# One expert block's gathers placed later in the GpSimd order, and a narrower rule for which PSUM accesses need no order

## The chip, the cores and the metric

The kernel runs on one core of one Trainium2 chip. The metric is the device time of one execution in microseconds (us). Three runs of the kernel before gave 913.91, 916.37 and 916.81 us, the median being 916.37 us.

## The reference

Attention comes first: 8 batches, 8 heads, 576 tokens of 64 dimensions, with rotary embedding on q and k. Its output, laid out as 4608 tokens of 512 values, goes through a mixture of 8 experts that picks one expert a token:

```python
scores = scale * np.matmul(q_rot, k_rot.transpose(0, 1, 3, 2))
attn = np.exp(scores - max); attn = attn / (sum + 1e-09)
x = (attn @ v).transpose(0, 2, 1, 3).reshape(4608, 512)
logits = x @ w_gate + modality_bias[modality_id]
e_idx = np.argmax(logits, axis=1); gate_w = softmax(logits)[e_idx]
for e in range(8):
    h = np.maximum(x[e_idx == e] @ w1[e], 0.0)        # 512 -> 1024
    out[e_idx == e] = gate_w * (h @ w2[e])            # 1024 -> 512
```

## The kernel before, in words

**Attention.** The 64 heads are worked as 32 pairs of heads, numbered 0 to 31, four pairs to a batch (so batch 5, the sixth in time, is pairs 20 to 23). A pair has nine score units S0 to S8. Each is a set of fp32r matmuls on TensorE into one PSUM slot (`scores`, matmul at L472), a pass of VectorE that copies the scores and takes the row minimum (`rowmin`, L481), and an exponential on ScalarE (`expo`, L490). The exponentials are then transposed on TensorE into PSUM by six fills: F0, F1, F2, F3, FA, FB (`fill`, `tpose`, L495). `evac` copies every fill out: the half g = 0, which is the first PSUM bank of the slot, on ScalarE (`acopy`, L432), the half g = 1, the second bank, on VectorE (`tensor_copy` at L528). F0 and F1 go to PH[0], F2 and F3 to PH[1], FA to PD[0]; FB is three copies an engine, into PH[1] and PD[1]. `AV` (L553) multiplies by V, half 0 (AVA) from PH[0], half 1 (AVB) from PH[1]. `avout` copies the result, `outp` (OUT, L590) turns it and computes the routing logits, `ev` (L603 to L607) scales it on VectorE.

**PSUM.** Attention has four slots, SL[0] to SL[3], each one tile of two banks. The table SLOTS says which unit takes which: F1 and F3 slot 3, F2 and S5 slot 0, F0, S8, S0 and OUT slot 1, FA, FB and S1 slot 2. `take` takes both banks of a slot (or one, for AV) and `give` hands a bank back.

**Which instructions wait for which.** The scheduler looks at the tiles that an instruction reads and writes and makes it wait for earlier instructions on other engines with which it shares a tile. `alone(own, b, inst)` is called by `evac`, `AV`, `avout` and `ev` for each access to bank b of slot `own`. It goes through the accesses recorded since the slot was taken, and for each of the other bank and of another engine it calls `declare_no_dep` with the reason "two banks": these two need no order.

**Order.** Every piece of work is a job with a key. The tables KEYS, EDGE (pairs with an order of their own: 0 to 4 and 26 to 31, and parts of 5 and 25) and MOE give the keys, and 14.438 times the pair is added. Jobs are sorted by key, and TensorE, ScalarE, VectorE, GpSimd and the DMA queue of SyncE each execute their instructions in that order. MOE's keys count from pair 31.

**Routing.** For each batch `route` picks the expert of each token; its last step casts the table rows `oi` on GpSimd (L697). `scatter` (L708) then writes a batch's token numbers and gates into TAB in DRAM, in five indirect DMAs of GpSimd, SC0 to SC4. Batches 0 to 4 make a first plan (`plan0`), in PLA: 8 expert blocks of 256 tokens that can begin before attention ends. `m_plan` loads a block's expert, row and flag from the plan into registers of SyncE (L932 to L934). `m_ix` issues two loads of the block's rows of TAB (ix at L944, xi at L946). `m_gather` computes addresses once a block (iy, L962) and issues eight indirect DMAs of GpSimd (L970) that fetch the tokens from X in DRAM into XG[s % 2]. A block's XG is transposed on VectorE (`m_tr`, L1015), split in high and low parts (`m_tre`), multiplied by w1 (`m_l1`, L1034), and by w2 (`m_l2`, L1053), and stored by an indirect DMA (L1057).

**Around the change.** Block 0's gathers run among pair 31's attention. Before the change block 1's plan values, index loads and gathers come next. On GpSimd its eight gathers stand directly behind block 0's last one, with the multiplication of `route` (L689) between them, and ahead of the cast `oi` of batch 5 and its five scatters, in the order SC3, SC4, SC2, SC1, SC0.

Of the kernel before, what the change touches and what calls it, by code (L numbers as in the profile page):

```python
# [194 lines left out]
MOE = dict(  # L195
    setdma=(-353.070, -199.654, -64.082, -129.156),
    consts=(28.166, 28.282),
    plan=(-34.727, 11.672, -5.857, -25.884),
    ix=(-13.525, 11.677, 11.679, 11.775),
    w1=(-33.501, -27.735, 15.231, -22.655),  # L200
    w2=(-4.011, 1.762, 12.647, -8.483),
    hi=(-22.046, 1.027, 19.870, 16.903),
# [6 lines left out]
    l1e=(22.809, 22.869, 24.662, 24.647),  # L209
    w1n=(20.502, 24.643, 23.254, 22.825),  # L210
    place=(10.490, 11.490),
    rows=(5.189, -7.595, 2.778, 1.170, -0.984, 8.071, 5.429, 11.766, 11.780, 11.790, 14.020, 14.030, 14.040, 14.050, 14.060, 14.070,
        25.150, 25.160, 25.170, 25.180, 25.190, 25.200, 25.210, 25.220),
    pl=(-114.356, -102.856, -99.906, -88.406, -85.506, -73.956, -51.417, -48.907, -45.303),
    end=25.0,
# [6 lines left out]
def tile_attention_moe(ctx: ExitStack, tc: tile.TileContext, qk, v, mod, wg, mb, w1, w2, rope, cf, ci, out):  # L222
    nc = tc.nc
# [75 lines left out]
    def take(nm, bks):  # L299

        own = SLOTS[nm]
        if nm == "RK8":
            own, bks = own & 3, (own >> 2,)
        if not all((own, b) in idle for b in bks):
            if nm == "RK8":
                own, b = min(idle, key=idle.get)
                bks = (b,)
            else:
                own = min((i for i in range(4) if all((i, b) in idle for b in bks)), key=lambda i: max(idle[i, b] for b in bks))
        for b in bks:  # L310
            del idle[own, b]
        if len(bks) == 2:
            use[own] = []
        return (own, *bks) if nm == "RK8" else own

    use = {}

    def alone(own, b, inst):

        for x, i in use[own]:  # L320
            if x != b and i.engine != inst.engine:
                tc.declare_no_dep(inst, i, reason="two banks")
        use[own].append((b, inst))

    def give(own, *bks):
        for b in bks:
            idle[own, b] = clock[0]
            clock[0] += 1
# [192 lines left out]
    def evac(n, f, g):  # L521
        d = st[n]
        ps = d[f][:, g]
        give(d["at", f], g)


        def cp(o, i):
            alone(d["at", f], g, (nc.vector.tensor_copy if g else acopy)(o, i).ins)  # L528

        if f[1] in "0123":  # L530
            h, o = divmod(int(f[1]), 2)
            o = o * P + g * 64
            cp(PH[h][:, :, o:o + 64], ps.rearrange("p (a b) -> p a b", b=64))
            return
        tails = PD[f == "FB"][:, 0:256].rearrange("p (j s c) -> p j s c", s=2, c=64)[:, :, g, :]
        if f == "FA":
            cp(tails, ps[:, 0:128].rearrange("p (j c) -> p j c", c=64))
        else:
            cp(PH[1][:, 4 * g:4 * g + 4, 256:320], ps[:, 0:256].rearrange("p (k c) -> p k c", c=64))
            cp(PD[1][g * 64:g * 64 + 64, 256:320], ps[g * 64:g * 64 + 64, 256:320])  # L540
            cp(tails, ps[:, 320:448].rearrange("p (j c) -> p j c", c=64))


    def AV(n, half):
        d = st[n]
        c0, c1 = (0, 256) if half == 0 else (256, 576)
        own = take("AV" + "AB"[half], (half,))
        pa = d["pa", half] = SL[own][:, half, :]
        d["at", "av", half] = own
        for kt in range(5):  # L550
            for hh in range(2):
                r = PH[half][:, 4 * hh + kt, :] if kt < 4 else PD[half]
                i = nc.tensor.matmul(pa[hh * 64:hh * 64 + 64, 0:c1 - c0], d["V"][:, hh, kt, :], r, start=(kt == 0), stop=(kt == 4))  # L553
                alone(own, half, i.ins)
                d.setdefault(("av", half), i.ins)

    def avout(n, half):
        d = st[n]
        c0, c1 = (0, 256) if half == 0 else (256, 576)
        own = d.pop(("at", "av", half))  # L560
        alone(own, half, acopy(OT[n % 2][:, c0:c1], d.pop(("pa", half))[:, 0:c1 - c0]).ins)
        give(own, half)
# [603 lines left out]
    for n in range(NPAIR):  # L1166
# [11 lines left out]
        for w in range(2):  # L1178
            c = "AB"[w]
            K_(f"AV{c}", AV, n, w)  # L1180
            K_(f"OT{c}", avout, n, w)
            K_(f"EV{c}", ev, n, 1 - w)
# [12 lines left out]
        if n % 4 == 3:  # L1195
            K_("BIAS", bias, n // 4)
            K_("XO", xout, n // 4)
            g = route(n // 4)
            steps = [(next, g, None)] * (NRK - (n == z))
            scats = [(scatter, n // 4, j) for j in range(5)]  # L1200
            if n == z:

                g = plan()
# [22 lines left out]
    g = plan0()  # L1226
# [201 lines left out]
```

## Time and profile before

| | us |
|---|---|
| median of three runs | 916.37 |
| the profiled execution's own time | 911.67 |
| its span, first to last instruction | 909.9 |
| TensorE busy | 863.7 |
| TensorE weight loads busy | 715.4 |
| VectorE busy | 685.8 |
| GpSimd busy | 641.1 |
| ScalarE busy | 632.3 |

The profile is one execution. PE is TensorE's matmuls, PEld its weight loads, DVE VectorE, ACT ScalarE, POOL GpSimd, SP SyncE with its DMA queue SPq. A row of the timeline gives start and length in us, the engine, the line of the kernel, the operation, the tiles as out<-in without their numbers, and the count of merged instructions; in brackets stands the idle time ahead of it with what ended that. "issue" there means that the engine waited for nothing that the profile shows. Attention lasts from the start to about 476 us, and the expert blocks from then to the end.

### The profile page before, as it was taken

What the parts mean: (1) busy time and instruction counts of PE and PEld (TensorE: products, weight loads), DVE (VectorE), ACT (ScalarE), POOL (GpSimd) and SP (SyncE); (2) the same over time, 40 slices, a digit from 0 to 9 for tenths busy, and PEclk for the clock granted to TensorE, in tenths of its full rate; (3) what the DMA queues carried; (4) which work ended last, traced back from release to release, by engine and by line L of the source; (5) the groups of instructions that cost most, each with busy time, mean ns of one, the idle gap of its engine ahead of it and who ended that gap; (6) DMA issues with size and microseconds to landing.
All of it is one profiled execution on the core that took longest, in us unless ns stands there. A gap on an engine that the chain in (4) does not pass through costs nothing. (4 is left out here: it accounts for less than half of the span.)

```text
span 909.9 us, 25743 instructions
## 1 busy us (share of the span) xinstructions
PE 863.7 (95%) x9696; PEld 715.4 (79%) x9696; DVE 685.8 (75%) x1515; ACT 632.3 (69%) x1291; POOL 641.1 (70%) x494
## 2 busy tenths in 40 slices
PE   2899999999999999999869989999999999999996
PEld 2677777777777777777648978889999999999995
DVE  7788889888888889888739767857676666666672
ACT  2888988888988988989734545556556555555563
POOL 3999988998889999995551776765666666666401
PEclk9999999999999999999969999999999999999999
DMA  8675778788797787867601611116717112511250
GB/s 263 200 225 156 247 180 219 182 207 204 151 246 181 190 207 182 230 166 215 171 21 67 222 49 46 54 59 228 237 55 229 47 47 88 192 46 38 81 171 20
DMA packets 82465, 136.90 MB, mean 150 GB/s; under 512 B 28795, under 2 KB 53517, under 8 KB 81308
## 3 DMA queue, kind: packets, MB, share of 16 engines
q1 hardware_dynamic: 71740, 114.08, 46.5%
q0 software_dynamic: 9248, 19.46, 6.6%
q8 instruction: 78, 1.28, 0.6%
q10 hardware_dynamic: 1344, 1.62, 0.6%
q14 instruction: 55, 0.45, 0.2%
HBM read 138.16 MB, written 19.51 MB: 173 GB/s over the span
## 5 line engine op out<-in xcount | busy, mean ns | idle before, releaser
L481 DVE CUSTOM_DVE_ANT_1 sc<-ps,ZERO 128x576 f32<-128x576 f32 x288 | 206.8, 749 | 23.3 <-PE ps L472 13.0
L490 ACT ACTIVATE P<-sc,mn 128x576 f32<-128x576 f32 x288 | 219.7, 767 | 5.8 <-DVE mn L481 5.2
L970 POOL DMA_INDIRECT XG<-X,iy x148 | 174.6, 1180 | 48.5 <-issue 37.6
L1034 PE MATMUL psH<-HL,W1H 128*128 128x256 f32 x1088 | 194.6, 281 | 3.2 <-issue 2.9
L472 PE MATMUL ps<-SW 64*128 64x288 f32 x960 | 170.3, 312 | 15.8 <-DMA SW<-HL 14.9
L472 PE MATMUL ps<-HL 64*128 64x288 f32 x960 | 170.6, 311 | 3.2 <-DVE ri L573 1.1
L1034 PEld LDWEIGHTS psH<-HL,W1H 128*128 128x128 f32 x1088 | 168.1, 189 | 4.0 <-issue 1.9
L1034 PE MATMUL psH<-HL,W1L 128*128 128x256 f32 x544 | 152.8, 281 | 0.9 <-issue 0.9
L472 PEld LDWEIGHTS ps<-SW 64*128 64x128 f32 x960 | 136.2, 190 | 20.6 <-DMA SW<-HL 15.9
L429 DVE TENSOR_TENSOR W1L<-ST,W1H 128x1024 fp32r<-128x1024 f32 x76 | 90.3, 1222 | 76.3 <-ACT W1H L432 65.5
L472 PEld LDWEIGHTS ps<-HL 64*128 64x128 f32 x960 | 136.2, 190 | 8.6 <-issue 5.5
L553 PE MATMUL ps<-PH,V 128*64 128x320 f32 (+1 forms) x1024 | 140.9, 416 | 2.2 <-issue 1.2
L1057 POOL DMA_INDIRECT out_dram<-sc,ix x36 | 47.0, 1305 | 115.3 <-ACT sc L1056 94.0
L495 PEld LDWEIGHTS ps<-idf,P 64*128 64x128 f32 x2624 | 96.8, 139 | 32.7 <-ACT P L490 12.1
L432 ACT ACTIVATE PH<-ps 128x512 f32<-128x512 f32 (+1 forms) x160 | 85.3, 551 | 48.5 <-PE ps L495 25.0
L528 DVE COPY PH<-ps 128x512 f32<-128x512 f32 (+1 forms) x160 | 98.4, 630 | 26.6 <-remote 12.8
L495 PE MATMUL ps<-idf,P 64*128 64x64 f32 x2624 | 109.1, 226 | 6.9 <-issue 3.5
L1053 PE MATMUL psY<-W2L,SW 128*128 128x512 f32 x288 | 113.7, 395 | 0.0
L1053 PE MATMUL psY<-W2H,SW 128*128 128x512 f32 x288 | 112.3, 390 | 0.0
L553 PEld LDWEIGHTS ps<-PH,V 128*64 128x64 f32 x1024 | 69.7, 137 | 51.3 <-issue 6.0
L449 POOL TENSOR_TENSOR HL<-ST,HL 128x1152 fp32r<-128x1152 f32 x31 | 82.4, 2657 | 36.6 <-ACT HL L432 36.5
L1034 PEld LDWEIGHTS psH<-HL,W1L 128*128 128x128 f32 x544 | 102.9, 189 | 3.8 <-issue 3.7
(216 smaller groups left out, 1596.7 us busy)
## 6 DMA issues: line engine op xcount, KB each, us to landing
ST<-in_moe_w_dram SPq DMA_DIRECT2D x152, 512.0 KB
ST<-in_qk_dram SPq DMA_DIRECT2D x62, 576.0 KB
SW<-HL SPq DMA_DIRECT2D x124, 216.0 KB
V<-in_v_dram SPq DMA_DIRECT2D x32, 256.0 KB
X<-X SPq DMA_DIRECT2D x8, 1024.0 KB
XG<-X,iy POOLq DMA_INDIRECT x148
V<-in_v_dram SPq DMA_DIRECT2D x64, 16.0 KB
X<-XT SPq DMA_DIRECT2D x16, 64.0 KB
```

What stands on the lines that cost most here:

```text
L429: nc.vector.tensor_tensor(o, a, b, op=ALU.subtract)
L432: return nc.scalar.activation(o, i, AF.Copy, scale=scale)
L449: e.tensor_tensor(d["HL"][:, 1, o], a, d["HL"][:, 0, o].bitcast(F32), op=ALU.subtract)
L472: nc.tensor.matmul(ps[:, g, 0:288], t[:, wq, q0:q0 + P], t[:, wk, k0:k0 + 288], start=(m == 0), stop=(m == len(L) - 1))
L481: nc.vector.tensor_tensor_reduce(sc, d.pop(("S", u))[:, :, 0:288], ZERO.unsqueeze(2).to_broadcast([P, 2, 288]), 1.0, FMAX, ALU.add, ALU.mi ...
L490: nc.scalar.activation(p, sc.rearrange("p a b -> p (a b)"), AF.Exp, bias=mn, scale=-1.0, accum_out=d["sum"][:, u:u + 1])
L495: nc.tensor.transpose(ps[:, g, c:c + 64], src[r, k0:k0 + P], idf[r, r])
L528: alone(d["at", f], g, (nc.vector.tensor_copy if g else acopy)(o, i).ins)
L553: i = nc.tensor.matmul(pa[hh * 64:hh * 64 + 64, 0:c1 - c0], d["V"][:, hh, kt, :], r, start=(kt == 0), stop=(kt == 4))
L970: inst = nc.gpsimd.indirect_dma_start(out=XG[s % 2][:, t, g, :], out_offset=None, in_=X.rearrange("n (i f) -> (n i) f", f=P)[0:rows], in_o ...
L1034: l1_[s] = nc.tensor.matmul(ps[:, i, :], w[:, c, f0:f0 + P], x[:, c, :], start=(m == 0), stop=(m == 11)).ins
L1053: nc.tensor.matmul(ps, hx[:, c, t * P:(t + 1) * P], x[:, c, :], start=(m == 0), stop=(m == 23))
```

## The change

Two things change. First, block 1's plan values move from key 11.672 to 16.183, its index loads from 11.677 to 17.300, and its eight gathers from 11.780 to 14.070 to 17.360 to 17.430. Batch 5's scatters stand at 15.355 (SC3), 16.855 (SC4), 17.438 (SC2), 21.457 and 22.004, counted in the same way. So on GpSimd the cast `oi` and two scatters come ahead of the eight gathers, and three scatters behind them; on SyncE's queue the plan values and the index loads come behind the index loads of blocks 2 and 3 and behind w1's third quarter of block 0 (15.231), and ahead of w1's first quarter for block 1 (20.502).

Second, `alone` takes a `part`, and no longer declares two accesses free of order when both have the same part. `evac` passes 0 for F0, F1 and FA, and 1 for F2, F3 and FB; `AV` passes its half; `avout` and `ev` pass none.

```diff
-    plan=(-34.727, 11.672, -5.857, -25.884),
-    ix=(-13.525, 11.677, 11.679, 11.775),
+    plan=(-34.727, 16.183, -5.857, -25.884),
+    ix=(-13.525, 17.300, 11.679, 11.775),
...
-    rows=(5.189, -7.595, 2.778, 1.170, -0.984, 8.071, 5.429, 11.766, 11.780, 11.790, 14.020, 14.030, 14.040, 14.050, 14.060, 14.070,
+    rows=(5.189, -7.595, 2.778, 1.170, -0.984, 8.071, 5.429, 11.766, 17.360, 17.370, 17.380, 17.390, 17.400, 17.410, 17.420, 17.430,
...
-    def alone(own, b, inst):
-
-        for x, i in use[own]:
-            if x != b and i.engine != inst.engine:
+    def alone(own, b, inst, part=None):
+
+        for x, p, i in use[own]:
+            if x != b and i.engine != inst.engine and (p is None or p != part):
                 tc.declare_no_dep(inst, i, reason="two banks")
-        use[own].append((b, inst))
+        use[own].append((b, part, inst))
...
-            alone(d["at", f], g, (nc.vector.tensor_copy if g else acopy)(o, i).ins)
+            alone(d["at", f], g, (nc.vector.tensor_copy if g else acopy)(o, i).ins, int(f[1] in "23B"))
...
-                alone(own, half, i.ins)
+                alone(own, half, i.ins, half)
```

## The prediction

> **What bounds the kernel now.** I read the page first (span, busy time, chain of waits), then the busy time of the attention stretch, then the timelines of the places that the diff touches.
>
> ```profile
> span 909.9 us, 25743 instructions
> ## 1 busy us (share of the span) xinstructions
> PE 863.7 (95%) x9696; PEld 715.4 (79%) x9696; DVE 685.8 (75%) x1515; ACT 632.3 (69%) x1291; POOL 641.1 (70%) x494
> ...
> q8 instruction: 78, 1.28, 0.6%
> ...
> PE 36%; issue 1%; POOL 1%; ACT 0%; DVE 0%; DMA 0%; POOLq 0%; ACTq 0%
> ```
> ```profile
> 97.00:355.00 258.00, 255.38 (x4172) 194.12 (x4171) 222.13 (x665) 227.23 (x585) 233.45 (x152) 1.00 0.81 196
> ```
>
> TensorE bounds it: 95% busy, and nearly all that the chain names. In the attention stretch from 97 to 355 us (pairs 5 to 23, 19 of them, so 13.6 us a pair) it is busy for 255.38 of 258.00 us, in full clock. The columns behind are weight loads, VectorE with 222.13 (86%) and ScalarE with 227.23 (88%). So there is no idle time on TensorE into which a new wait could sink: what delays its next matmul there is paid, unless it makes a later wait shorter.
>
> **The second edit: the two copies of a fill.** I take this one first because it acts in every pair. In `evac` both copies of a fill have the same slot, different banks, different engines, and now the same part, so the new test is false for every such pair and "two banks" is no longer declared. The declaration was there to take away an order: the two copies share the PSUM tile of the slot, though neither its banks nor the columns that they write. Without it I expect the later one in program order to wait for the earlier. It is the only thing that `declare_no_dep` can have removed between them. The keys say who is first: ScalarE in F0, F1, F2, FA and FB, VectorE in F3 (13.72 against 13.92).
>
> Here is one pair's crowded place, FB, F3 and F2, on ScalarE, then VectorE, then TensorE, each from its timeline:
>
> ```profile
> 306.39 0.26 ACT L432 ACTIVATE PD<-ps 128x128 f32<-128x128 f32 x1
> 306.56 0.60 ACT L432 ACTIVATE PH<-ps 128x512 f32<-128x512 f32 x1
> 306.56 1.09 ACT L432 ACTIVATE PH<-ps 128x512 f32<-128x512 f32 x2
> ```
> ```profile
> 306.00 0.42 DVE L528 COPY PH<-ps 128x256 f32<-128x256 f32 x1 [0.29 <-PE ps L495]
> 306.89 0.68 DVE L528 COPY PH<-ps 128x512 f32<-128x512 f32 x1
> 307.49 0.68 DVE L528 COPY PH<-ps 128x512 f32<-128x512 f32 x1
> 308.08 0.75 DVE L481 CUSTOM_DVE_ANT_1 sc<-ps,ZERO 128x576 f32<-128x576 f32 x1
> 308.76 0.08 DVE L481 DVE_READ_ACCUMULATOR2_ANT mn<- 128x1 f32 x1
> ```
> ```profile
> 307.72 0.71 PE L495 MATMUL ps<-idf,P 64*128 64x64 f32 x16
> 308.21 0.38 PE L472 MATMUL ps<-SW 64*128 64x288 f32 x1
> ...
> 309.12 0.29 PE L472 MATMUL ps<-SW 64*128 64x288 f32 x1
> ...
> 309.60 1.30 PE L553 MATMUL ps<-PH,V 128*64 128x320 f32 x8
> ```
>
> Now the copies run side by side. Walked again with the order put in, with 0.04 us for a release to arrive (VectorE's F2 copy ends at 307.49 + 0.68 = 308.17, and the next TensorE work starts at 308.21):
>
> - FB: ScalarE's third copy ends at 306.39 + 0.26 = 306.65, so VectorE's first starts at 306.69, not 306.00: 0.69 late.
> - F3: VectorE's copy moves from 306.89 to 307.58 and ends at 308.26. ScalarE's waits for it and starts at 308.30, not 306.56: 1.74 late. It ends at 308.90.
> - F2: ScalarE's copy follows in the old distance (1.09 for two, 0.60 for one, so 0.49 apart), at 308.79, to 309.39. VectorE's starts at 309.43, not 307.49: 1.94 late.
> - The minimum of S8 stands right behind it on VectorE: 308.08 becomes 310.02, and its result is out at 308.84 + 1.94 = 310.78.
> - TensorE: the next pair's F1 needs slot 3, which ScalarE's F3 copy leaves at 308.90, so 307.72 becomes 308.94 (1.22 late). The last scores of this group, S0, need slot 1, which the minimum of S8 frees: about 309.10 (one matmul ahead of the row at 309.12) becomes 310.82. That is 1.72 late, and AVB, at 309.60, is late with it.
>
> A second place is F0, whose slot OUT takes next:
>
> ```profile
> 300.72 0.58 ACT L432 ACTIVATE PH<-ps 128x512 f32<-128x512 f32 x1
> ```
> ```profile
> 300.78 0.69 DVE L528 COPY PH<-ps 128x512 f32<-128x512 f32 x1
> ```
> ```profile
> 301.62 0.60 PE L590 MATMUL ps<-RW,oT 64*64 64x72 f32 x23
> ```
>
> VectorE's copy would start at 301.34 and end at 302.03, and OUT at 302.07: 0.45 late at most. A TensorE that is late already gives ScalarE time to be there sooner, so I take 0.2. The copies of FA (0.26 us) and of F1 (VectorE comes there after the late minimum) I take at nothing: the work on VectorE ahead of them covers that; uncovered, F1's would cost one ScalarE copy, 0.6, and FA's 0.26, and they stay inside the upper bound of the other pairs below.
>
> Per pair 1.72 + 0.2 = 1.92 us. From below it is 1.22 (F1's fill alone, all else caught up), from above 1.72 + 0.45 = 2.17. Nineteen pairs have this order: 19 x 1.92 = 36.5 us (23 to 41). The other 13 have orders of their own (in pair 27 the keys set F0's copies 0.95 apart, for instance); there the bounds are 0 and 13 x 2.17 = 28, and I take a good quarter, 8, since their copies stand further apart. Sum of this edit: **+44.5 us**, bounds 23 and 69. The other new effect, AVB waiting for ScalarE's F3 copy, I cost at 0: AVB stands in the order behind F2's copies, which on ScalarE come after F3's in the usual order.
>
> By the Trainium skill, "PSUM — Partial Sum Buffer", section "Specifications (TRN2)", ScalarE and VectorE can read PSUM in parallel at full bandwidth as long as the bank differs. The rows at 300.72 and 300.78 agree. By that rule the chip needs no order here and the sum would be 0; but it is the program that waits.
>
> **The first edit: where the move lands.** Rows of TensorE around it, its usual pace for the same three pieces of work, then GpSimd, VectorE and SyncE's queue:
>
> ```profile
> 455.20 0.71 PE L590 MATMUL ps<-RW,oT 64*64 64x72 f32 x13
> ...
> 461.39 0.37 PE L590 MATMUL ps<-RW,oT 64*64 64x72 f32 x1 [1.05 <-issue]
> ...
> 473.09 0.76 PE L553 MATMUL ps<-PD,V 128*64 128x256 f32 x4
> ```
> ```profile
> 450.51 0.86 PE L590 MATMUL ps<-RW,oT 64*64 64x72 f32 x36
> 451.33 0.72 PE L495 MATMUL ps<-idf,P 64*128 64x64 f32 x16
> ```
> ```profile
> 303.00 1.95 PE L553 MATMUL ps<-PH,V 128*64 128x256 f32 x16
> 304.78 0.60 PE L553 MATMUL ps<-PD,V 128*64 128x256 f32 x4
> ```
> ```profile
> 451.13 0.99 POOL L970 DMA_INDIRECT XG<-X,iy  x1 [1.45 <-PE ps L590]
> 452.76 1.06 POOL L970 DMA_INDIRECT XG<-X,iy  x1 [0.27 <-POOL iy L962]
> ...
> 462.12 0.99 POOL L970 DMA_INDIRECT XG<-X,iy  x1 [0.30 <-issue]
> 463.12 0.20 POOL L697 CAST oi<-of 128x5 int32<-128x5 f32 x1
> 463.60 1.03 POOL L708 DMA_INDIRECT TAB<-VAL,oi  x1 [0.28 <-issue]
> ...
> 468.74 0.97 POOL L708 DMA_INDIRECT TAB<-VAL,oi  x1 [0.30 <-issue]
> 491.08 0.19 POOL L697 CAST oi<-of 128x5 int32<-128x5 f32 x1 [21.37 <-DVE of L694]
> ```
> ```profile
> 460.11 0.15 DVE L694 TENSOR_REDUCE of<-rk 128x5 f32<-128x40 f32 x1
> ...
> 492.74 1.28 DVE L1015 STREAM_TRANSPOSE XG<-XG 128x512 f32<-128x512 f32 x2
> ```
> ```profile
> 449.12 33.47 SPq L986 DMA_DIRECT2D ST<-in_moe_w_dram  x5
> ```
> ```profile
> L932 SPq TENSOR_LOAD <-PLA x4: 267/279/475, 404.5 to 442.0; - x4
> ```
>
> Moved past each other, the eight gathers and two scatters cost GpSimd the same 1.30 us each. The cast can start when `of` is there, at 460.26. Two scatters then end at about 463.2, the iy and eight gathers at 474, three scatters at 478, where they ended at 469.7. Block 1's tokens are first read at 492.74, 18 us later, and GpSimd's next work is at 491.08: both hide it, and without that cover each us late would be a us on the block 1 split. On SyncE three plan loads (0.28 each and registers) and two issues now stand behind the first w1 quarter of the row at 449.12 and ahead of one that waits until 477 anyway: nothing.
>
> What the move may change is the hole. OUT, a fill and AVA take 18.65 us from 455.20 to 473.85, where the usual pace is 0.86 + 0.72 + 2.38 = 3.96: **14.7 us are lost**, in "issue" time that names no releaser, while GpSimd issues one indirect DMA after another. After the move GpSimd has none between block 0's last gather at 451.13 + 0.99 and the cast. Whether the hole goes with the gathers the trace cannot say. Against it speaks a later stretch in which GpSimd (the fifth engine in the row, busy 15.95 of 20.00 us) gathers for another block:
>
> ```profile
> 500.00:520.00 20.00, 20.00 (x141) 18.29 (x140) 16.96 (x28) 12.95 (x17) 15.95 (x15) 1.00 0.73 238
> ```
>
> TensorE is busy in all of its 20.00 us. I take 0 and keep 0 to -14.7.
>
> By the Trainium skill, "Runtime: NRT & Kernel Launch", section "Instruction fetch mechanics", an engine refills its instructions in 16 KiB blocks by a DMA queue of its own; q8's 78 packets in 1.28 MB are such blocks. By that rule the hole would be TensorE's own and stay, and the sum would be +44.5; if it were the gathers', +29.8.
>
> **Sum.** 911.67 + 44.5 = 956.2 us for the profiled execution; the median of the runs stands 4.70 above that execution, so 960.9, said as 961.
>
> **The rivals.**
>
> - The hole closes as well: 961 - 14.7 = **946**. For it: the hole lies inside the run of gathers. Against: the stretch from 500 us, and that they only move some 8 us on, beside the first expert matmuls.
> - It ends on the other side if no wait comes with the copies, the scheduler telling the two banks apart by itself, and the hole closes: 916.4 - 14.7 = **902**. It decides from the point where the copies cost less than 14.7 / 32 = 0.46 us a pair. Against it: then the declaration in the kernel before would have had no use.
> - Neither happens, and the change does nothing: **916**.
> - The other 13 pairs pay in full and F0 too, 69 us: **986**.
>
> **How the numbers follow.** The forecast (copies wait, hole stays) 0.50, the hole closing as well 0.30, faster 0.07, no change 0.06, worse than 985 0.07. The forecast's own range is 940 to 985. The range of all that I hold to 8 in 10 takes in the second case, whose middle is 946 and which reaches down to some 936: 936 to 985. About 0.3% is what a measurement of this kernel can tell from no change. Faster by more than that: 0.08; within it: 0.05; slower: 0.87.
>
> **What would show it.** In the profile after, F3's copy on ScalarE starts after VectorE's has ended, F2's on VectorE after ScalarE's; the waits name DVE PH for ACT PH and the reverse; pairs 5 to 23 take about 15.5 us each and TensorE falls to some 87% in that stretch. The first edit is right if OUT and AVA of pair 31 take as long as now, wrong if they take 4 us. The whole is wrong if the two copies still start together.

## The result

The kernel after takes **961.74 us** in the median of four runs (952.75 to 964.91) beside 915.14 for the kernel before (908.49 to 916.81): a ratio of 1.0508, with a 95% interval of 1.0433 to 1.0583. It is slower. The profiled execution took 952.75 us, with a span of 951.0 where before had 909.9, so 41.1 us more.

From the page of the kernel after: the span, the busy time, the chain that ended last by engine, and two of the costliest groups, the copies of a fill on VectorE and on ScalarE (line, operation, count, then busy us and mean ns of one, then the idle time ahead of them and what ended most of it).

```profile
span 951.0 us, 25629 instructions
PE 878.1 (92%) x9696; PEld 714.9 (75%) x9696; DVE 687.5 (72%) x1515; ACT 639.2 (67%) x1291; POOL 654.4 (69%) x494
PE 74%; DVE 9%; ACT 8%; issue 5%; DMA 1%; POOL 1%; ACTq 0%; POOLq 0%; DVEq 0%
L528 DVE COPY PH<-ps 128x512 f32<-128x512 f32 (+1 forms) x160 | 100.7, 633 | 67.8 <-ACT PH L432 44.5
L432 ACT ACTIVATE PH<-ps 128x512 f32<-128x512 f32 (+1 forms) x160 | 85.1, 550 | 62.3 <-DVE PH L528 32.5
```

The same two groups in the kernel before:

```profile
L528 DVE COPY PH<-ps 128x512 f32<-128x512 f32 (+1 forms) x160 | 98.4, 630 | 26.6 <-remote 12.8
L432 ACT ACTIVATE PH<-ps 128x512 f32<-128x512 f32 (+1 forms) x160 | 85.3, 551 | 48.5 <-PE ps L495 25.0
```

The copies are as long as before (633 against 630 ns, 550 against 551). What is new is whom they wait for: VectorE's copies were held for 44.5 us by ScalarE's, ScalarE's for 32.5 us by VectorE's. And the chain goes 9% over VectorE and 8% over ScalarE. The chain of before that the prediction shows can't be laid beside it, since it reaches back only to 552.33 us, behind attention. In a second profile of before (below, on the first chip) the chain covers nearly the whole span, with 2% and 4% in the same two places:

```profile
PE 90%; ACT 4%; DVE 2%; DMA 1%; another core or an unknown queue 1%; issue 1%; ACTq 0%; POOLq 0%; POOL 0%; DVEq 0%
```

The same crowded place as in the prediction, FB, F3 and F2 of a pair, in the timelines of ScalarE, then VectorE, then TensorE of the kernel after:

```profile
344.45 0.38 ACT L432 ACTIVATE PH<-ps 128x256 f32<-128x256 f32 x1 [0.16 <-PE ps L495]
346.80 1.09 ACT L432 ACTIVATE PH<-ps 128x512 f32<-128x512 f32 x2 [1.69 <-DVE PH L528]
```
```profile
345.13 0.42 DVE L528 COPY PH<-ps 128x256 f32<-128x256 f32 x1 [0.87 <-ACT PD L432]
345.57 0.53 DVE L528 COPY PD<-ps 64x64 f32<-64x64 f32 x2
346.02 0.68 DVE L528 COPY PH<-ps 128x512 f32<-128x512 f32 x1
347.91 0.69 DVE L528 COPY PH<-ps 128x512 f32<-128x512 f32 x1 [1.21 <-ACT PH L432]
```
```profile
340.07 0.86 PE L590 MATMUL ps<-RW,oT 64*64 64x72 f32 x36 [0.37 <-DVE PH L528]
...
347.45 0.72 PE L495 MATMUL ps<-idf,P 64*128 64x64 f32 x16 [1.18 <-ACT PH L432]
...
349.94 2.37 PE L553 MATMUL ps<-PH,V 128*64 128x320 f32 x16
```

It reads as a staircase. ScalarE copies its part of FB, then VectorE its own (from 345.13), then VectorE F3 (346.02 to 346.70), then ScalarE F3 and F2 (346.80 to 347.89), then VectorE F2 (347.91). No two copies of one fill overlap any more. TensorE pays 1.18 us ahead of F1's fill and 0.37 ahead of OUT.

The second place is the stretch behind the last OUT but one, where before lost 14.7 us (TensorE of the kernel after):

```profile
512.85 1.48 PE L590 MATMUL ps<-RW,oT 64*64 64x72 f32 x36
514.26 0.80 PE L495 MATMUL ps<-idf,P 64*128 64x64 f32 x16
514.99 1.95 PE L553 MATMUL ps<-PH,V 128*64 128x256 f32 x16
516.76 0.60 PE L553 MATMUL ps<-PD,V 128*64 128x256 f32 x4
```

OUT, the fill and AVA take 4.5 us where they took 18.65. **The hole has closed.** (The prediction calls it pair 31's OUT; by the keys it is an earlier pair's, which changes nothing in the times.)

So the traces, laid against each other at the same pieces of TensorE's work, give in us:

| | before | after | difference |
|---|---|---|---|
| start to OUT of pair 4 | 97.7 | 100.7 | +3.0 |
| OUT of pair 4 to OUT of pair 23, 19 pairs | 258.2 | 302.3 | +44.1 |
| from there to the last OUT but one | 99.3 | 109.9 | +10.6 |
| from there to the first expert matmul | 21.3 | 7.1 | -14.2 |
| from there to the end | 433.4 | 431.0 | -2.4 |
| span | 909.9 | 951.0 | +41.1 |

The copies cost 57.7 us, 14.2 came back at the hole, and 2.4 behind it. The last figure hangs on this one trace of before: a second one took 426.3 us there in place of 433.4.

### The profile page after: what moved, and what is told of

Same layout as the page of the kernel before. It is cut to its first block, busy times and chain, and to the rows that moved or that the text cites. A ratio compares the mean times of both kernels' runs of the same rounds, so it can differ in the third digit from the quotient of the medians.

```text
span 951.0 us, 25629 instructions
## 1 busy us (share of the span) xinstructions
PE 878.1 (92%) x9696; PEld 714.9 (75%) x9696; DVE 687.5 (72%) x1515; ACT 639.2 (67%) x1291; POOL 654.4 (69%) x494
## 3 DMA queue, kind: packets, MB, share of 16 engines
q8 instruction: 78, 1.28, 0.6%
## 4 chain that ended last, share of the span: by engine, by line
PE 74%; DVE 9%; ACT 8%; issue 5%; DMA 1%; POOL 1%; ACTq 0%; POOLq 0%; DVEq 0%
PE psH L1034 20%; PE psY L1053 20%; PE ps L553 16%; PE ps L472 10%; DVE PH L528 6%; PE ps L495 5%; ACT PH L432 4%; PE ps L590 2%; ACT P L490 2%; DVE PD L528 1%; DVE sc L481 1%; POOL XG L970 1%; ACT PD L432 1%; PE psY L1094 1%; ACT HL L432 1%
## 5 line engine op out<-in xcount | busy, mean ns | idle before, releaser
L970 POOL DMA_INDIRECT XG<-X,iy x148 | 192.2, 1299 | 51.5 <-issue 36.9
L481 DVE CUSTOM_DVE_ANT_1 sc<-ps,ZERO 128x576 f32<-128x576 f32 x288 | 206.1, 748 | 15.5 <-PE ps L472 8.6
L472 PE MATMUL ps<-SW 64*128 64x288 f32 x960 | 184.3, 318 | 16.7 <-DMA SW<-HL 12.7
L472 PE MATMUL ps<-HL 64*128 64x288 f32 x960 | 185.0, 318 | 6.9 <-ACT PH L432 2.2
L528 DVE COPY PH<-ps 128x512 f32<-128x512 f32 (+1 forms) x160 | 100.7, 633 | 67.8 <-ACT PH L432 44.5
L429 DVE TENSOR_TENSOR W1L<-ST,W1H 128x1024 fp32r<-128x1024 f32 x76 | 90.3, 1222 | 74.5 <-ACT W1H L432 49.8
L432 ACT ACTIVATE PH<-ps 128x512 f32<-128x512 f32 (+1 forms) x160 | 85.1, 550 | 62.3 <-DVE PH L528 32.5
```

Of the source, the lines that this page charges most:

```text
L429: nc.vector.tensor_tensor(o, a, b, op=ALU.subtract)
L432: return nc.scalar.activation(o, i, AF.Copy, scale=scale)
L472: nc.tensor.matmul(ps[:, g, 0:288], t[:, wq, q0:q0 + P], t[:, wk, k0:k0 + 288], start=(m == 0), stop=(m == len(L) - 1))
L481: nc.vector.tensor_tensor_reduce(sc, d.pop(("S", u))[:, :, 0:288], ZERO.unsqueeze(2).to_broadcast([P, 2, 288]), 1.0, FMAX, ALU.add, ALU.mi ...
L970: inst = nc.gpsimd.indirect_dma_start(out=XG[s % 2][:, t, g, :], out_offset=None, in_=X.rearrange("n (i f) -> (n i) f", f=P)[0:rows], in_o ...
```

## The experiments

The first four kernels ran on one chip, on which the kernel before took 914.05 us; the next four on a second chip (before: 886.15), the last four on a third (before: 885.11). That the same kernel is 3% quicker on two chips turned out to matter, so each table row below names the chip by the time of before on it. The table gives the same stretches as above, from each kernel's own trace.

| kernel | before on this chip | to OUT of pair 4 | 19 pairs | to the last OUT but one | to the first expert matmul | to the end | span |
|---|---|---|---|---|---|---|---|
| before, again | 914 | 97.5 | 257.9 | 99.2 | 18.3 | 426.3 | 899.2 |
| part alone | 914 | 103.0 | 300.9 | 109.5 | 20.8 | 426.1 | 960.3 |
| move alone | 914 | 97.0 | 258.3 | 102.1 | 6.4 | 428.9 | 892.7 |
| copies free | 914 | 97.7 | 258.9 | 99.6 | 6.4 | 431.6 | 894.1 |
| F2, F3, FB ordered | 886 | 100.9 | 290.9 | 103.3 | 6.7 | 430.7 | 932.5 |
| F3 swapped | 886 | 102.0 | 279.2 | 102.7 | 6.7 | 429.5 | 920.1 |
| four gathers early | 886 | 96.8 | 256.9 | 96.1 | 6.4 | 427.1 | 883.5 |
| scatters late | 886 | 96.6 | 258.4 | 95.9 | 6.4 | 426.5 | 883.8 |
| after, again | 885 | 101.9 | 299.3 | 106.4 | 6.7 | 431.4 | 945.8 |
| before, again | 885 | 96.2 | 256.6 | 96.6 | 6.4 | 426.1 | 882.0 |
| move, again | 885 | 98.4 | 256.4 | 97.8 | 6.4 | 429.0 | 888.0 |
| F0, F1, FA ordered | 885 | 97.0 | 272.2 | 98.3 | 6.4 | 430.2 | 904.1 |

### Which edit costs what

**The part alone.** The kernel before with the new `alone`, nothing moved.

```diff
...
-            if x != b and i.engine != inst.engine:
+            if x != b and i.engine != inst.engine and (p is None or p != part):
...
```

> The kernel before with the new part of alone and nothing moved. Theory (the copies of a fill wait for each other): TensorE waits for PH of ScalarE at F1's fill (1.2 us) and for PH of VectorE at OUT (0.4 us) in each of pairs 5 to 23, 15.8 us a pair; 58 us more up to pair 30's OUT, as the profile after shows between the same two places. If the slow stretch of pair 31 comes from the eight gathers on GpSimd beside it, it stays, and the time is about 915 + 58 = 973; if not, about 959. Rival (the move costs the time): 915.

Measured: 964.38 us, ratio 1.0578 (1.0496 to 1.066). All of the loss is there with the move left out: 300.9 us for the 19 pairs, and 5.5 and 10.3 more around them than in the second profile of before. The hole stands too (20.8). The 973 added the 58 us of one pair of traces to the median of before. Span against span, the part alone is 61.1 us longer than the second profile of before and 50.4 longer than the first, which has 7 us more behind the first expert matmul (433.4 against 426.3). So executions of before differ by more than the miss, and the pairs show no smaller price of the copies.

**The move alone.** The kernel before with the new MOE keys (the plan values, the index loads and, in `rows`, the eight gathers) and the old `alone`.

```diff
-    plan=(-34.727, 11.672, -5.857, -25.884),
-    ix=(-13.525, 11.677, 11.679, 11.775),
+    plan=(-34.727, 16.183, -5.857, -25.884),
+    ix=(-13.525, 17.300, 11.679, 11.775),
...
```

> The kernel before with block 1's plan values, index loads and gathers moved, and the old alone. Theory: pairs 5 to 23 stay at 13.6 us; if the slow stretch of pair 31 comes from the gathers beside it, it closes, and the time is 915 - 14 = 901; if not, 915. Rival (the move costs the time): about 960.

Measured: 902.88 us, ratio 0.9883 (0.9835 to 0.993), where the theory had 901. By itself the first edit takes 1.2% off on this chip, and the 19 pairs stay at 258.3.

**Copies free.** The kernel after, with the order taken from the copies of one fill alone.

```diff
-            if x != b and i.engine != inst.engine and (p is None or p != part):
+            if x != b and i.engine != inst.engine and (p is None or p != part or mybir.EngineType.PE not in (i.engine, inst.engine)):
```

> The kernel after, but two copies of one fill are still declared free of order; only a copy and a matmul of AV with the same part are not. Theory (the order between the two copies is the cost): as with the move alone, 901 to 915, pairs of 13.6 us. Rival (the cost is AVA or AVB waiting for copies of its part): about 960, pairs of 15.8 us, with the waits at AVA and AVB.

Measured: 894.4 us, ratio 0.9776 (0.9703 to 0.9848), 258.9 for the 19 pairs. The order between AV and the copies of its part costs nothing that can be seen; the order between the two copies is the whole loss. On this chip it is the quickest version tried, ahead of both kernels. The move alone should be its like, and in the profiles it is (894.1 and 892.7). But that profile of the move is one of the two fastest of six runs (894.47 and 894.63; the other four 901.67 to 905.2), so what parts the two medians, 8.5 us, stays open.

### Which copies

**F2, F3 and FB ordered**, the others free (second chip).

```diff
-            if x != b and i.engine != inst.engine and (p is None or p != part):
+            if x != b and i.engine != inst.engine and (p is None or p != part or (part == 0 and mybir.EngineType.PE not in (i.engine, inst.engine))):
```

> The kernel after, with the copies of F0, F1 and FA declared free of order again, so that only those of F2, F3 and FB wait for each other. Theory (FB, F3 and F2 in a row are the costly place, 1.9 us of a pair at F1's fill and at S0, and OUT's wait of 0.37 us is F0's): the waits of 1.2 us for ScalarE's PH stay, those at OUT go, pairs of 15.4 to 15.5 us, about 894 + 19 x 1.9 + 8 = 938. Rival (any two ordered copies cost the same, so half of the cost is with F0, F1 and FA): 926 to 930, pairs of 14.7.

Measured: 935.41 us, ratio 1.0556 (1.0527 to 1.0584), so 49.3 us; the 19 pairs take 290.9 against 256.9 in a variant of before on the same chip, **1.79 us a pair**. A pair takes 15.31 us, which is close to the theory's 15.4 to 15.5 and far from the rival's 14.7. OUT no longer waits. TensorE at F1's fill:

```profile
322.85 0.71 PE L495 MATMUL ps<-idf,P 64*128 64x64 f32 x16 [1.19 <-ACT PH L432]
```

**F0, F1 and FA ordered**, the others free (third chip), the same line with `part == 1`.

> The kernel after, with the copies of F2, F3 and FB declared free of order again, so that only those of F0, F1 and FA wait for each other: the other half of the run in which only F2, F3 and FB did. Theory (F0's copy delays OUT by 0.4 us, F1's and FA's are hidden): pairs 0.2 to 0.45 us longer than in before, 32 x 0.3 = 10 us more than the move alone. Rival (F1's order delays S4's minimum behind it and costs as much as F3's): 25 us or more.

Measured: 905.05 us, ratio 1.0221 (1.0194 to 1.0249), so 19.9 us, and (272.2 - 256.6) / 19 = **0.82 us a pair**. That is nearly twice the upper end of 0.45 that I gave these fills. Against the move on the same chip it is 16.6 us, between the theory's 10 and the rival's 25. The two halves, each against before on its own chip, come to 49.3 + 19.9 = 69.2 us, where the kernel after loses 65.1: between them they hold the whole loss. TensorE and VectorE in one pair:

```profile
311.61 0.86 PE L590 MATMUL ps<-RW,oT 64*64 64x72 f32 x36 [0.38 <-DVE PH L528]
...
319.88 2.38 PE L553 MATMUL ps<-PH,V 128*64 128x320 f32 x16 [0.22 <-DVE PH L528]
```
```profile
319.14 0.69 DVE L528 COPY PH<-ps 128x512 f32<-128x512 f32 x1 [0.31 <-ACT PH L432]
```

OUT waits 0.38 us for F0's copy, and AVB, which takes slot 3 after F1, waits 0.22 for F1's copy on VectorE. The prediction had put this second one at nothing. In the 19 pairs OUT waits 7.3 us in all and AVB 4.6, and two waits that name no releaser, of 1.0 and 0.7 us, stand in the two longest pairs. That is 13.6 of the 15.6 us that these pairs lost; the rest is in no wait that the profile lists.

**F3 swapped.** The kernel after with one key changed, so that VectorE waits for ScalarE in F3 (second chip).

```diff
-    ... "A_F3": 13.92, "B_F3": 13.72, ...
+    ... "A_F3": 13.70, "B_F3": 13.72, ...
```

> The kernel after, with the key of ScalarE's copy of F3 ahead of VectorE's (13.70 against 13.72; on each engine the order stays), so that VectorE waits for ScalarE there. Theory, walked as in the prediction: ScalarE's copy of F3 is no longer late, F1's fill waits for nothing, VectorE's copies of F3 and F2 start at the end of ScalarE's, S8's minimum and S0 are 0.85 us late in place of 1.9: 19 x 1.05 = 20 us less than after, about 941. Rival (it is the number of waits, not their sense): 961, pairs of 15.8.

Measured: 923.19 us, ratio 1.0417 (1.0384 to 1.0449), so 37.0 us over before where the kernel after is 65.1 over it on the third chip: 28 us come back for one key, where the walk had 20 and the rival none. A pair takes (279.2 - 256.9) / 19 = 1.17 us more than in before. ScalarE, VectorE and TensorE:

```profile
327.47 1.10 ACT L432 ACTIVATE PH<-ps 128x512 f32<-128x512 f32 x2
```
```profile
328.47 1.28 DVE L528 COPY PH<-ps 128x512 f32<-128x512 f32 x2
```
```profile
329.21 0.71 PE L495 MATMUL ps<-idf,P 64*128 64x64 f32 x16 [0.49 <-DVE PH L528]
```

Both engines now run F3 and F2 without a gap. One step of the walk was still wrong: I had F1's fill wait for nothing, but slot 3 needs VectorE's half of F3 as well, and that half stands behind VectorE's late copies of FB: 0.49 us.

### The hole

**Before, again**, on the first chip, for a second profile.

> The kernel before, unchanged, for a second profile of it. If the 14.7 us in which TensorE issues slowly at OUT, F and AVA of pair 31 belong to the program, they stand in this profile too, at the same three pieces of work, and the time is 912 to 917 us. If they are an event of one execution, that stretch takes about 4 us here, or the slow stretch stands elsewhere, and the time is about 902.

Measured: 901.1 us in its one execution. It is neither forecast: the hole is there, at the same place, in another shape and 3 us shorter (18.3 in the table against 21.3). That the time is near the 902 of the second forecast is luck: 7 us are gone behind the first expert matmul as well, where neither forecast put any.

**Four gathers early** and **scatters late** were for its cause: the kernel before with block 1's last four gathers moved, and the kernel before with batch 5's scatters made to wait for AVB (both on the second chip). In the second, SC3, the first of the five, is made to wait, its key moves from 130.859 to 131.950, and the other four follow it on GpSimd.

```diff
-... 11.766, 11.780, 11.790, 14.020, 14.030, 14.040, 14.050, 14.060, 14.070,
+... 11.766, 11.780, 11.790, 14.020, 14.030, 17.390, 17.400, 17.410, 17.420,
```
```diff
...
+        if (b, j) == (5, 3): tc.add_manual_dep(inst, st[31]["av", 1].name, ...)
```

> The kernel before, with only the last four of block 1's gathers moved behind batch 5's first two scatters. If the gathers beside OUT, F and AVA of pair 31 slow TensorE's issue one by one, the slow stretch is about half as long, 7 us, and the time about 907. If what slows it is that GpSimd issues indirect DMAs then at all, gathers or scatters, it stays at 14 us, and the time is 914.

> The kernel before, with batch 5's five scatters made to wait for the first matmul of AVB of pair 31, and the gathers left where they were. If the gathers alone slow TensorE, the slow stretch ends with the last of them, some 8 us after its start, and about 6 of the 14 us come back: 908. If the scatters do, it closes: 901. If neither matters, 914.

Measured: 886.78 us, ratio 1.0002 (0.9985 to 1.0019), and 885.25, ratio 0.9995 (0.9978 to 1.0012). Inconclusive, both: before itself takes 886.15 there, and neither trace has a hole that could shrink. So the last group asked about the chip.

> The kernel before, unchanged, for its profile on this chip. If the time of before is near 886, TensorE takes about 4 us for OUT, F and AVA of pair 31, at one go; if it is near 914, they take 15 to 19 us, in issue time.

> The move alone, beside the kernel before on the same chip. If the chip shows no slow stretch in before: 886, the same within 0.3%. If it does: 11 to 14 us less than before.

> The kernel after, unchanged, beside the kernel before on the same chip. On the chip of the runs just seen, the kernel before took 886 us and the profiles of its two variants show no slow stretch at pair 31; there the move has nothing to win, and the order of the copies alone remains: 886 + 58 = 944, 6.5% more than before. On the chip of the earlier runs: 961, 5% more.

Measured on the third chip: before again 883.78 us; the move again 888.44, ratio 1.0039 (1.0014 to 1.0064), a little outside the 0.3% expected; after again 950.22, ratio 1.0742 (1.0724 to 1.076), where 944 was expected. TensorE and GpSimd of before on this chip, at the place of the hole:

```profile
449.44 0.86 PE L590 MATMUL ps<-RW,oT 64*64 64x72 f32 x36
450.22 0.71 PE L495 MATMUL ps<-idf,P 64*128 64x64 f32 x16
450.86 1.95 PE L553 MATMUL ps<-PH,V 128*64 128x256 f32 x16
452.64 0.60 PE L553 MATMUL ps<-PD,V 128*64 128x256 f32 x4
```
```profile
450.44 1.05 POOL L970 DMA_INDIRECT XG<-X,iy  x1 [0.16 <-issue]
451.79 1.00 POOL L970 DMA_INDIRECT XG<-X,iy  x1 [0.30 <-issue]
```

The gathers run right beside OUT, the fill and AVA, and TensorE takes 3.8 us for them, at one go. So the hole stood only where two things met: a chip of the first sort (the runs of the result, with 915.14 us for before, count with it: 18.3 to 21.3 us from that OUT to the expert matmuls in all three traces with the gathers there, 6.4 to 7.1 in all three without) and the gathers beside it. Two scatters alone did not make one: in the kernel after they run beside AVA and AVB (516.27 and 517.63). The move shifts the plan values and index loads too, but in before these had landed by 447.74 us, 7 us ahead of the hole. No run on the first chip moved the gathers by themselves, so that it is they is argued and not isolated. On the other two chips the stretch takes 6.4 to 6.7 us in every kernel.

What differs between the chips was not settled. Each was used in one session, so the chip and the hour can't be told apart. The granted clock over the runs of before was 0.977 to 0.981 on the first chip and 0.993 to 0.998 on the other two. In the hole itself it was 0.60 (before), 0.72 (before again) and 0.59 (the part alone), against 0.88 in the kernel after and 1.00 in the move alone, which had no hole. Estimated from these figures, a clock of 0.60 makes 6.3 us of 3.8 and not 18.65, and whether it is a cause of the hole or comes of it no run shows. The traces show one mark of it: in the hole ScalarE and VectorE wait too, for a release that the profile can give to no instruction of the core. From the waits of before (the first result) and of before again on the first chip: total us, times, longest.

```profile
ACT PH L432 <- remote: 14.0, 2, 12.4
DVE PH L528 <- remote: 12.8, 2, 11.3
```
```profile
ACT PH L432 <- remote: 11.3, 1, 11.3
DVE PH L528 <- remote: 10.1, 1, 10.1
```

In before again the fill's last matmuls of this place start at 458.21, and both engines' copies of that fill start at 466.82. It is thus not only TensorE's own issue that is slow there; the release of its readers comes late as well. Every trace of a chip of the first sort lists such remote waits. The ones without the hole have shorter ones behind it, none over 3.8 us, but in sum not always less: 5.2 us with the copies free, 8.6 for the move alone, 14.0 for the kernel after (at L1042 and L1056); none of the eight traces of the second and third chip lists any.

**What the move costs where there is no hole.** On the third chip the move loses 3.3 us in the median. VectorE, TensorE and GpSimd of the move again, and VectorE's work beside the long gather:

```profile
475.07 0.69 DVE L1015 STREAM_TRANSPOSE XG<-XG 128x512 f32<-128x512 f32 x1
480.03 0.71 DVE L1015 STREAM_TRANSPOSE XG<-XG 128x512 f32<-128x512 f32 x1 [4.27 <-DMA XG<-X,iy]
```
```profile
483.89 0.50 PE L1034 MATMUL psH<-HL,W1H 128*128 128x256 f32 x2 [1.38 <-ACT W1H L432]
485.21 0.58 PE L1034 MATMUL psH<-HL,W1L 128*128 128x256 f32 x1 [0.83 <-DVE W1L L429]
```
```profile
461.12 5.16 POOL L970 DMA_INDIRECT XG<-X,iy  x1 [0.31 <-issue]
...
475.09 1.00 POOL L970 DMA_INDIRECT XG<-X,iy  x1 [0.30 <-issue]
```
```profile
461.83 1.21 DVE L429 TENSOR_TENSOR W2L<-ST,W2H 128x1024 fp32r<-128x1024 f32 x1
...
464.17 1.20 DVE L429 TENSOR_TENSOR W2L<-ST,W2H 128x1024 fp32r<-128x1024 f32 x1
```

Block 1's last gather is issued at 475.09, and VectorE stands 4.27 us for its tokens. Behind it on VectorE and ScalarE are the splits of block 1's weights, and TensorE waits 1.38 + 0.83 = 2.2 us for them. The kernel after has the same two waits in the trace of the result (1.25 and 0.82 us).

## Why the prediction was right, and where it was not

The time (961 against 961.74), the sign and the main mechanism were right. The closeness of the sum is luck, and a reader should not take it for more. The copies cost 13.2 us more than the 44.5 put in, 14.2 came back at the hole and 2.4 behind it where 0 was put in, and the median after stands 8.99 us above the profiled execution where the sum added before's 4.70. So the profiles differ by 41.1 us, not 44.5, and the median's 4.3 make up for that.

- **The two copies wait for each other.** Right, and tested: with this order alone the loss is all there, with it taken away it is gone.
- **The walk through FB, F3 and F2.** Right in its steps. For the walked pair F1's fill is 1.28 us later (7.38 after OUT in place of 6.10) where 1.22 was forecast, and AVB another 0.61 where 0.50 was. OUT's own wait is 0.36 to 0.46 in the trace, and since the walked pair had some slack it lengthened it by 0.20, the value that I took. The walked pair comes to 15.77 - 13.68 = 2.09 us, against 1.92.
- **Nineteen times the walked pair.** Here the term was mis-sized. In before the pairs alternate between 13.3 and 13.7 us, and I had walked one of the longer ones. The shorter ones have no slack, and pay OUT's wait in full: 13.30 becomes 15.64, of which 0.45 is OUT's. F1's copy, taken at nothing, costs AVB 0.22 us when nothing else holds AVB, as the run with F0, F1 and FA ordered shows. On the third chip the mean is (299.3 - 256.6) / 19 = 2.25 us. The first chip's trace has 2.32, with two pairs of 17.25 and 17.50 us in it, in which the granted clock was 0.90 where the pair ahead of them had 1.00 (the clock is the third figure from the end):

```profile
163.70:180.90 17.20, 15.59 (x218) 10.81 (x218) 11.57 (x36) 12.17 (x32) 12.25 (x8) 0.90 0.69 169
```

  The 19 pairs cost 44.1, not 36.5, and lie above my upper end of 41; so do the 42.7 of the third chip, which has no such pair. The 2.17 a pair from which that end came was too low: the short pairs lose 2.34.
- **The other 13 pairs.** 8 us taken, 13.6 measured (3.0 ahead and 10.6 behind), inside 0 to 28. Together the copies cost 57.7 us where the sum had 44.5. (By the terms of the sum, 69 us on top come to 985.4 and not to 986.)
- **The hole stays, 0.** Wrong on this chip: 14.2 us came back. The stretch from 500 us, in which gathers and expert matmuls ran together, was what spoke for 0; that gathers leave TensorE alone in one place did not show that they do in the other. What I had held at 0.30, that the hole closes as well, is what happened; its time of 946 was too low mainly by the copies' larger price, 13.2 of the 15.7 us. The reading by which the hole is TensorE's own and stays is out with it.
- **The gathers are late, and hidden.** Wrong by 2 us, 1.25 + 0.82 in the kernel after. I had 1.30 us for every indirect DMA from a trace in which VectorE had next to nothing to do beside them (in the hole it waited 11.3 us at one go); beside VectorE's work one of them takes 5.16. And most of the 18 us of cover were the hole's: with it closed, the first read of block 1's tokens comes sooner.
- **AVB behind ScalarE's F3 copy, 0.** Right: with the copies free and this order kept, the 19 pairs take 258.9.
- **"Nearly all that the chain names" is TensorE.** True of the row, but that chain covers the expert blocks alone (from 552.33 us), so it says nothing of attention. The row of 97 to 355 us, TensorE busy for 255.38 of 258.00, carries the argument by itself.
- **SyncE's queue, nothing.** No run shows a cost there; the expert loads were not isolated.

On a chip without the hole nothing offsets the copies, and the kernel after is 65 us slower (1.0742). The forecast's +4.9% belongs to the first sort of chip.

## What to carry to other kernels

Before taking away a declared independence, ask which pairs of instructions lose it beside those that one meant: here the new order was wanted, if at all, between copies and matmuls, and it caught two copies that read different banks on different engines. When one period is walked to price a wait, walk the one without slack, and multiply by that. A stall that names no releaser may belong to the chip or the session: a second profile of the kernel before, on another chip, is a cheap experiment. And when a sum comes out right, lay its terms against the traces one by one.

## What the runs showed of the hardware

The same kernel took 914 us on one chip and 885 to 886 on two others. Of the 27.9 us between the spans 909.9 and 882.0, 14.9 lie in the one stretch described above, and 7.3 behind it; but a second execution on the first chip had none of these 7.3 (426.3 us behind the first expert matmul, against 426.1 on the third chip).

An indirect DMA that GpSimd issues in 1.00 us took 5.16 while VectorE ran one L429 subtraction after another (461.83 to 465.37), and was done 0.9 us after the last of them. The kernel before on the third chip has the same: 4.47 us from 458.66, with L429 from 458.71 to 462.26. Who begins first seems to decide it. In that trace the gather at 457.37, begun ahead of a subtraction (457.58), took 0.99 us, and the one at 455.17, begun inside a subtraction that ended at 456.19, took 1.90 and ended 0.88 us behind it:

```profile
455.17 1.90 POOL L970 DMA_INDIRECT XG<-X,iy  x1 [0.30 <-issue]
457.37 0.99 POOL L970 DMA_INDIRECT XG<-X,iy  x1 [0.30 <-issue]
```
```profile
454.94 1.25 DVE L429 TENSOR_TENSOR W1L<-ST,W1H 128x1024 fp32r<-128x1024 f32 x1
457.58 1.20 DVE L429 TENSOR_TENSOR W1L<-ST,W1H 128x1024 fp32r<-128x1024 f32 x1
```

The Trainium skill, "SBUF — State Buffer", section "Who interferes with whom", says that a VectorE instruction with two SBUF inputs holds up a GpSimd instruction that reads SBUF, and that VectorE operations of L429's kind were not seen to stall DMAs issued from GpSimd. L429 reads two tiles, and an indirect DMA reads its row numbers from a third. The traces agree with the first sentence; for the indirect DMAs of this kernel they speak against the second. No run here took the subtractions away, so the cause is argued and not shown.
